# Sliding-window attention and token mixing on one core: exponential over 192 columns per head and key block, scores in 64x64 pieces

## The chip, the cores and the metric

The kernel runs on one core of a Trainium2 chip. The metric is the device time of one execution in microseconds (us); the median of the runs before the change is 136.63 us (136.03 to 137.59, 3 runs). [...]

## The reference

Eight batches, eight heads, 576 tokens, 64 elements per head. A query sees the 128 keys that end at itself, with a bias that falls linearly with the distance and has a slope for each head. The heads' outputs, side by side, are the x of a token mixer.

```python
scores = scale * np.matmul(q, k.transpose(0, 1, 3, 2))
rel = pos[:, None] - pos[None, :]
bias = slopes[:, None, None] * (-np.abs(rel).astype(np.float32))[None, :, :]
mask = (rel >= 0) & (rel < window)          # window = 128
scores = np.where(mask, scores + bias[None], -1000000000.0)
attn = np.exp(scores)                       # divided by its row sum
attn_out = np.matmul(attn, v)
# mixer: x is attn_out as (batch, 576, 512)
W_tok = scale * np.einsum('bsd,btd->bst', x @ w_q, x @ w_k)
mixed = np.einsum('bst,btd->bsd', W_tok, x)
out = np.maximum(mixed, 0.0) @ w_out
```

## The kernel before, in words

**Order.** The order of all work is written out by hand in the table ORDER (line 42). A word such as `QK4.0.1:P:3` names an operation (batch 4, key block 0, half 1 of the heads), its engine (P is PE, A is ACT, V is DVE, G is POOL, S is SP) and, for PE, the PSUM banks; a further number is a count of filler matmuls that go ahead of it. Each engine takes its words from left to right and waits in place for what an operation needs.

**Per batch.** `L...` load q, k and v by POOL's queue (at most some 6 us of transfers at a time), `FQ` the first q heads by SP's. `TW` (batches 0 to 3), `TN` (4 to 7) and `TT` (the last 64 tokens of two batches) transpose q and k on PE; `ETW`, `ETN`, `ETT` on ACT or DVE copy the result from PSUM to `qkT`. `QK` makes the scores, `EXP` (line 608) exponentiates them, `MUL` (line 621) multiplies by exp(bias) with zeros where a key isn't seen, `PV` multiplies by v, and `X` (lines 662 and 663, DVE) divides by the row sum. Then `XT`/`EXT` transpose x, `WK`, `WQ`, `G`, `MX` with `EWK`, `EWQ`, `EG`, `GX`, `RM` on ACT or DVE are the mixer, and `OUT`, `EO`, `DO` multiply by w_out, copy and store.

**Scores (`add_unit`, line 562).** A unit is one key block of 128 keys (g = 0 to 3; g = 3 also holds the last 64 keys) for four heads (u = 0 or 1): 64 units. Keys are the rows of the result, queries its columns. For a full key block and one head a matmul with 64 contraction rows and 128 result rows makes 128 keys by 256 queries: the block's own 128 queries, then the next 128. The two heads e = 0 and 1 of a pair lie in the upper and the lower 64 rows of the array and write to two banks. Of the 256 columns a key uses 128, so half of what `EXP` computes is multiplied by zero. `EXP` writes 1024 columns per unit to `pt` (a ring of 5), `MUL` works in place, for a whole key block (2048 columns) except in batch 0. `EXP` waits until the `PV`s that read the ring's slot five blocks ago are done.

**Forms of the array.** PE's matmuls come in three forms, given in the profile as rows*columns: 128*128 (`PV`, `WK`, `OUT`, filler), 64*128 (`QK`, `TN`, `TT`, `XT`, `MX`) and 128*64 (`TW`, `WQ`, `G`, `OUTb.4`). All matmuls are recorded at line 207, the transposes at 210, the fillers at 908, copies from PSUM mostly at 222, 224, 228 and 230.

Of the kernel before, what the change touches and what calls it, by code (L numbers as in the profile page):

```python
# [1 line left out]

# [16 lines left out]
H = 8  # L19
# [8 lines left out]
NPT = 5  # L28

# [13 lines left out]
FQ1:S FQ0:S Lk0.0:G CQ1:A ones4:V ident:G iota:G dist:V zerop:V zeros:V CQ0:V idh:V perm:V  # L43
Lq0.1:G mask:G bias0:A Lk0.1:G bias1:A ones1:V TW0.0:P:0:15 ETW0.0.0:A ETW0.0.1:V
QK0.1.0:P:0:4:1 QK0.2.0:P:1 EXP0.1.0:A EXP0.2.0:A QK0.0.0:P:2 TW0.1:P:3:1:3 pads:V ones3:V
ones0:V ETW0.1.1:V Lt0.2:G Lt0.3:G ETW0.1.0:A QK0.0.1:P:3:4:0 Lt0.0:G Lt0.1:G QK0.1.1:P:1
QK0.2.1:P:0 EXP0.0.0:A Lq1.1:G Lk1.1:G EXP0.0.1:A EXP0.1.1:A Lq1.0:G EXP0.2.1:A Lk1.0:G Lv0.0:G
Lv0.1:G Lv0.2:G TT0:P:2 ETT0:V ETT1:A QK0.3.1:P:3 QK0.3.0:P:1 Lv0.3:G EXP0.3.0:A TW1.1:P:2:1:0
ETW1.1.0:A MUL0.2.0:V MUL0.0.0:V biasl1:V MUL0.1.0:V MUL0.0.1:V EXP0.3.1:A ETW1.1.1:V
QK1.0.1:P:2:4:0 EXP1.0.1:A QK1.1.1:P:1 Lwq:G Lv0.4:G TW1.0:P:3:2:0 ETW1.0.1:A Lv1.0:G ETW1.0.0:A  # L50
Lwk:G Lq2.1:G biasl0:V MUL0.3.0:V MUL0.1.1:V MUL0.2.1:V MUL0.3.1:V PV0.0:P:2 X0.0:V Lk2.1:G
Lt1.0:G Lv1.1:G PV0.1:P:0:2:0 EXP1.1.1:A Lq2.0:G X0.1:V QK1.1.0:P:3 EXP1.1.0:A PV0.2:P:2 X0.2:V
Lk2.0:G ones2:G QK1.0.0:P:0 EXP1.0.0:A PV0.3:P:1 QK1.3.0:P:2 PV0.4:P:3 X0.3:V XT0.1:P:1
XT0.0:P:0 X0.4:V EXT0.0:V EXP1.3.0:A EXT0.1:A QK1.2.1:P:2 EXP1.2.1:A XT0.2:P:30 EXT0.2:V
MUL1.0:V QK1.2.0:P:1 MUL1.1:V QK1.3.1:P:0 EXP1.3.1:A Lv1.2:G WK0:P:30 MUL1.3:V EWK0:A WQ0:P:20
EWQ0:A Lv1.3:G PV1.0:P:0 X1.0:V G0:P:30 TW2.1:P:2 EXP1.2.0:A PV1.1:P:1 X1.1:V Lv1.4:G Lt1.2:G
EG0:A GX0:A Lt1.1:G MX0.0:P:3 RM0.0:V Lt1.3:G MUL1.2:V MX0.1:P:0 ETW2.1.1:A ETW2.1.0:A MX0.2:P:2
QK2.1.1:P:1 RM0.1:A RM0.2:A QK2.0.1:P:0 XT1.0:P:3 EXT1.0:V EXP2.0.1:A TW2.0:P:2 ETW2.0.0:V
PV1.2:P:0 X1.2:V EXP2.1.1:A ETW2.0.1:A Lq3.0:G QK2.2.1:P:3 PV1.3:P:1 X1.3:V EXP2.2.1:A
QK2.0.0:P:2 PV1.4:P:0 MX0.3:P:3 EXP2.0.0:A RM0.3:A XT1.1:P:1 TT1:P:2 ETT2:A Lk3.1:G Lq3.1:G  # L60
Lk3.0:G Lv2.0:G X1.4:V ETT3:V XT1.2:P:00 EXT1.2:A QK2.2.0:P:3 QK2.1.0:P:2 EXT1.1:V EXP2.2.0:A
QK2.3.0:P:0 WK1:P:10 EXP2.1.0:A QK2.3.1:P:3 MUL2.0:V EWK1:V EXP2.3.1:A MUL2.2:V MUL2.1:V
WQ1:P:11 EWQ1:A Lv2.1:G Lv2.2:G Lv2.3:G G1:P:10 EG1:A Lv2.4:G TW3.1:P:2 ETW3.1.0:V MX1.0:P:1
EXP2.3.0:A MUL2.3:V ETW3.1.1:A RM1.0:A TW3.0:P:3 ETW3.0.1:A ETW3.0.0:A PV2.0:P:2 X2.0:V
QK3.0.1:P:1 EXP3.0.1:A Lk4.1:G Lk4.0:G PV2.1:P:0 X2.1:V QK3.0.0:P:3 GX1:S EXP3.0.0:A Lwo.0:G
PV2.2:P:2 X2.2:V QK3.1.1:P:1 EXP3.1.1:A PV2.3:P:0 X2.3:V QK3.3.0:P:3 EXP3.3.0:A PV2.4:P:2 X2.4:V
Lwo.1:G XT2.0:P:1 EXT2.0:A XT2.1:P:0 EXT2.1:A QK3.3.1:P:3 EXP3.3.1:A Lv3.4:G Lt2.1:G Lwo.2:G
Lwo.3:G Lq4.1:G Lq4.0:G XT2.2:P:20 EXT2.2:V Lk4.2:G Lv3.1:G Lq4.2:G TN4.1.0:P:1 QK3.2.1:P:0
EXP3.2.1:A ETN4.1.0:V Lv3.0:G Lq4.3:G WK2:P:20 EWK2:V Lk4.3:G MX1.1:P:3 RM1.1:V QK3.1.0:P:1
EXP3.1.0:A WQ2:P:21 G2:P:20 EG2:A EWQ2:V MX1.2:P:3 RM1.2:A MX1.3:P:1 RM1.3:V QK3.2.0:P:0 Lv3.2:G  # L70
EXP3.2.0:A GX2:V Lv3.3:G OUT0.3:P:21 EO0.3:A OUT1.3:P:10 EO1.3:A MX2.2:P:0 MX2.0:P:2 MUL3.3:V
RM2.0:A RM2.2:V TN4.0.0:P:3 MUL3.0:V ETN4.0.0:A OUT1.2:P:11 EO1.2:A Lt2.0:G Lk5.1:G Lq5.3:G
MX2.3:P:0 RM2.3:A MX2.1:P:2 MUL3.1:V RM2.1:A QK4.0.1:P:3 EXP4.0.1:A Lk5.0:G OUT0.0:P:10 EO0.0:A
Lq5.1:G Lq5.0:G Lt2.3:G Lt2.2:G PV3.0:P:0 X3.0:V OUT1.0:P:11 EO1.0:A QK4.0.0:P:2 TN4.0.1:P:3
EXP4.0.0:A ETN4.0.1:V TN4.1.1:P:0 ETN4.1.1:A OUT0.2:P:10 EO0.2:A PV3.1:P:3 QK4.1.1:P:2
EXP4.1.1:A Lv4.0:G Lv4.1:G Lk5.2:G Lq5.2:G Lk6.1:G Lk5.3:G Lv4.2:G MUL3.2:V X3.1:V PV3.2:P:0
X3.2:V Lv4.3:G Lv4.4:G QK4.1.0:P:1 QK4.2.1:P:3 EXP4.2.1:A EXP4.1.0:A PV3.4:P:2 OUT2.2:P:00
EO2.2:A X3.4:V MUL4.0:V PV3.3:P:3 X3.3:V TN5.1.0:P:2 ETN5.1.0:A QK4.2.0:P:1 XT3.2:P:01
EXP4.2.0:A EXT3.2:A OUT1.4:P:00 EO1.4:V TN5.0.0:P:2 ETN5.0.0:A TT2:P:3 ETT4:V ETT5:A XT3.0:P:1
EXT3.0:A MUL4.2:V MUL4.1:V XT3.1:P:0 EXT3.1:A QK4.3.1:P:2 QK4.3.0:P:3 EXP4.3.1:A EXP4.3.0:A  # L80
OUT2.0:P:10 PV4.0:P:0 X4.0:V WK3:P:11 PV4.1:P:2 X4.1:V EWK3:A EO2.0:A QK5.0.0:P:3 TN5.0.1:P:0
ETN5.0.1:V EXP5.0.0:A G3:P:11 EG3:A GX3:S MUL4.3:V Lq6.3:G Lv5.0:G WQ3:P:20 EWQ3:A Lv5.3:G
Lq6.1:G Lq6.2:G Lv5.4:G Lq6.0:G Lk6.0:G TN5.1.1:P:0 Lv5.1:G Lv5.2:G ETN5.1.1:A Lk6.3:G Lt3.3:G
QK5.0.1:P:1 XT4.0:P:3 EXT4.0:V PV4.2:P:2 QK5.1.0:P:0 X4.2:V EXP5.0.1:A PV4.4:P:3 X4.4:V
EXP5.1.0:A QK5.2.1:P:1 EXP5.2.1:A PV4.3:P:2 X4.3:V QK5.1.1:P:0 EXP5.1.1:A QK5.3.1:P:3 EXP5.3.1:A
OUT2.1:P:10 EO2.1:A MUL5.0:V MX3.0:P:0 RM3.0:V XT4.1:P:2 EXT4.1:A OUT0.1:P:11 XT4.2:P:10
EXT4.2:A MX3.3:P:0 RM3.3:A MX3.1:P:3 RM3.1:A MUL5.1:V EO0.1:V QK5.2.0:P:2 EXP5.2.0:A WK4:P:10
EWK4:V PV5.0:P:0 X5.0:V QK5.3.0:P:3 EXP5.3.0:A WQ4:P:10 MUL5.2:V G4:P:11 EG4:A GX4:S TN6.1.0:P:0
ETN6.1.0:A MX3.2:P:2 TN6.0.0:P:3 ETN6.0.0:A OUT1.1:P:11 EWQ4:V MUL5.3:V MX4.1:P:3 RM4.1:V
QK6.0.1:P:0 RM3.2:A EO1.1:A PV5.2:P:2 X5.2:V PV5.1:P:1 X5.1:V EXP6.0.1:A TN6.0.1:P:3 ETN6.0.1:A  # L90
# [24 lines left out]
DO6.2:S DO7.3:S EO7.1:V DO7.1:S DO7.0:S DO7.2:S OUT7.4:P:31 EO7.4:A DO7.4:S
# [22 lines left out]
def kernel(  # L138
# [805 lines left out]
```

## Time and profile before

| what | value |
|---|---|
| median of the runs | 136.63 us |
| the profiled execution | 136.72 us |
| its span in the profile | 134.9 us |
| PE busy | 124.2 us, 2353 matmuls |
| ACT busy | 114.8 us, of it `EXP` 63.5 us in 64 instructions |
| DVE busy | 110.0 us, of it `MUL` 38.7 us in 36 instructions |
| POOL busy | 101.0 us |
| granted PE clock | 1.0 |

The execution takes 1.8 us more than its span. Busy time of PE is a union of modelled, overlapping matmuls: a group's row in the timeline lasts until its last result is out, so the distance from one group's start to the next group's start is what a group really takes. "PEld" is the load of the matmul's stationary operand, which runs beside earlier matmuls.

### The profile page before, as it was taken

How to read it: one execution, taken by the hardware profiler on the slowest of the kernel's cores; microseconds unless marked ns; L12 is line 12 of the kernel's file. 1: busy time of each engine (PE TensorE's matmuls, PEld its weight loads, DVE VectorE, ACT ScalarE, POOL GpSimd, SP SyncE). 2: the span in 40 equal slices, each digit the busy share in tenths (PEclk: the TensorE clock that was granted, in tenths of full speed). 3: DMA queues.
4: the chain of work that ended last, by engine and by line, in shares of the span. 5: the costliest groups of instructions: out<-in, count | busy, mean ns of one | idle time of the engine just before them, and what ended most of it. 6: DMA issues, size and time to landing. Idle time of an engine off the chain costs nothing.

```text
span 134.9 us, 5537 instructions
## 1 busy us (share of the span) xinstructions
PE 124.2 (92%) x2353; PEld 81.9 (61%) x2353; DVE 110.0 (82%) x216; ACT 114.8 (85%) x182; POOL 101.0 (75%) x144
## 2 busy tenths in 40 slices
PE   6998599998998989999999999999999999999960
PEld 2355356786777766457688666666766656663420
DVE  3654989899999967988999999999998997973600
ACT  3767978999999989999999999979999897478450
POOL 6995898699497999999999999999880724370000
PEclk9999999999999999999999999999999999999999
DMA  3999999999999999999999999999999999876693
GB/s 109 187 132 178 185 157 161 173 178 125 165 187 151 176 152 146 155 148 148 135 149 145 159 156 148 152 140 147 234 286 232 297 198 329 287 284 254 227 381 91
DMA packets 93319, 25.12 MB, mean 186 GB/s; under 512 B 80368, under 2 KB 89840, under 8 KB 93296
## 3 DMA queue, kind: packets, MB, share of 16 engines
q0 software_dynamic: 89488, 19.28, 152.7%
q1 hardware_dynamic: 3808, 5.51, 12.3%
q8 instruction: 18, 0.29, 0.8%
q14 instruction: 5, 0.04, 0.1%
HBM read 29.62 MB, written 9.44 MB: 289 GB/s over the span
## 4 chain that ended last, share of the span: by engine, by line
PE 65%; ACT 10%; DVE 9%; issue 7%; DMA 4%; POOL 1%; POOLq 0%; DVEq 0%
PE pair L207 53%; PE pair L210 11%; ACT pt L608 5%; DMA natp<-in_k_dram 4%; DVE x L663 3%; DVE pt L621 2%; ACT rm L775 1%; DVE rm L777 1%; ACT qkT L494 1%; DVE inv L662 1%; DVE xtl L663 1%; ACT gs L222 1%; DVE gx L224 1%; ACT wkn L222 1%; ACT gx L222 1%
## 5 line engine op out<-in xcount | busy, mean ns | idle before, releaser
L608 ACT ACTIVATE pt<-pair 128x1024 f16<-128x1024 f32 x64 | 63.5, 1042 | 1.9 <-PE pair L207 1.7
L213 POOL DMA_DIRECT2D vt<-in_v_dram x40 | 36.7, 979 | 5.1 <-DMA natt<-in_k_dram 2.1
L621 DVE TENSOR_TENSOR pt<-pt,bias 128x2048 f16<-128x2048 f16 (+1 forms) x36 | 38.7, 1099 | 0.2
L207 PE MATMUL pair<-wout_sb,rm 128*128 128x512 f16 (+1 forms) x160 | 35.8, 381 | 0.0
L207 PE MATMUL pair<-qkT 64*128 64x256 f16 (+3 forms) x352 | 23.9, 243 | 1.3 <-ACT pt L608 1.0
L207 PE MATMUL pair<-vt,pt 128*128 128x65 f16 x576 | 23.8, 193 | 1.0 <-issue 0.5
L213 POOL DMA_DIRECT2D natp<-in_k_dram x24 | 23.1, 1009 | 1.6 <-POOLq L928 0.8
L207 PEld LDWEIGHTS <-pt 128*128 128x128 f16 x576 | 20.2, 97 | 6.7 <-issue 3.9
L663 DVE TENSOR_TENSOR x<-pair,inv 128x512 f16<-128x512 f32 x32 | 22.1, 692 | 1.1
L213 POOL DMA_DIRECT2D natp<-in_q_dram x23 | 22.3, 1007 | 0.0
L207 PEld LDWEIGHTS <-rm 128*128 128x128 f16 (+1 forms) x160 | 12.4, 100 | 12.9 <-issue 1.7
L222 ACT COPY natp<-pair 128x512 f32<-128x512 f32 x22 | 13.2, 600 | 6.7 <-PE pair L207 6.7
L216 POOL DMA_DIRECT2D out_dram<-natp x16 | 9.3, 614 | 11.2 <-ACT natp L222 10.7
L207 PEld LDWEIGHTS <-qkT 64*128 64x128 f16 x352 | 12.7, 94 | 6.3 <-issue 3.1
L210 PEld LDWEIGHTS <-natp 128*64 128x64 f16 (+1 forms) x512 | 12.6, 102 | 5.0 <-issue 3.5
L777 DVE TENSOR_SCALAR rm<-pair 128x576 f16<-128x576 f32 x14 | 10.4, 752 | 3.3 <-PE pair L207 2.6
L775 ACT ACTIVATE rm<-pair 128x576 f16<-128x576 f32 x18 | 11.4, 668 | 0.9 <-PE pair L207 0.8
L908 PE MATMUL pair<-fill 128*128 128x512 f16 x33 | 10.5, 453 | 1.7 <-DVE fill L350 1.2
L662 DVE RECIPROCAL inv<-pair 128x8 f32<-128x8 f32 (+1 forms) x40 | 8.1, 203 | 2.4 <-PE pair L207 1.6
L228 ACT COPY qkT<-pair 128x512 f32<-128x512 f32 (+1 forms) x18 | 9.2, 542 | 0.8 <-PE pair L210 0.6
L210 PE MATMUL pair<-permh,natp 128*64 128x128 f16 x256 | 8.8, 220 | 1.0 <-DMA natp<-in_k_dram 0.7
L494 ACT COPY qkT<-pair 128x512 f32<-128x512 f32 x11 | 6.2, 593 | 2.2 <-PE pair L210 2.1
(66 smaller groups left out, 154.2 us busy)
## 6 DMA issues: line engine op xcount, KB each, us to landing
vt<-in_v_dram POOLq DMA_DIRECT2D x32, 128.0 KB, 5.3
out_dram<-natp SPq DMA_DIRECT2D x16, 256.0 KB, 2.4
out_dram<-natp POOLq DMA_DIRECT2D x12, 256.0 KB, 4.5
natp<-in_k_dram POOLq DMA_DIRECT2D x8, 256.0 KB, 6.0
natp<-in_k_dram POOLq DMA_DIRECT2D x16, 128.0 KB, 4.8
natp<-in_q_dram POOLq DMA_DIRECT2D x16, 128.0 KB, 4.7
natp<-in_q_dram POOLq DMA_DIRECT2D x7, 256.0 KB, 5.4
out_dram<-osb POOLq DMA_DIRECT2D x4, 256.0 KB, 4.4
```

The source lines that it names most:

```text
L207: hold(nc.tensor.matmul(*a, **k))
L210: hold(nc.tensor.transpose(*a))
L213: hold(nc.gpsimd.dma_start(**k))
L216: i = (nc.gpsimd if eng == "POOL" else nc.sync).dma_start(**k)
L222: hold(nc.scalar.copy(out_ap, in_ap))
L608: nc.scalar.activation(out=pt[:, 1024 * u:1024 * u + 1024], in_=two(s.bank).rearrange("p e c -> p (e c)"), func=AF.Exp, scale=SCALE)
L621: nc.vector.tensor_tensor(out=pt[:, lo:hi], in0=pt[:, lo:hi], in1=bt[:, lo:hi], op=ALU.mult)
L662: nc.vector.reciprocal(out=inv[r], in_=pxv[r, :, :, 64])
L663: nc.vector.tensor_tensor(out=x[r].rearrange("p (g h d) -> p g h d", g=2, h=4), in0=pxv[r, :, :, 0:64], in1=inv[r].unsqueeze(3).broadcast_ ...
L775: hold(nc.scalar.activation(out=out_ap, in_=in_ap, func=AF.Relu, scale=WSCALE))
L777: hold(nc.vector.tensor_scalar(out=out_ap, in0=in_ap, scalar1=0.0, scalar2=WSCALE, op0=ALU.max, op1=ALU.mult))
L908: nc.tensor.matmul(where[:, half, :], fill[:, 0:P], fill, start=True, stop=True)
```

## The change: what it does

In a full key block the first 64 keys need the queries 0 to 190 of the 256, and the last 64 keys the queries 64 to 254. The scores of a head are therefore kept in 192 columns: the upper 64 result rows (first keys) hold queries 128 to 191 in columns 0 to 63 and queries 0 to 127 in columns 64 to 191; the lower 64 rows (last keys) hold queries 128 to 255 in columns 0 to 127 and queries 64 to 127 in columns 128 to 191. Each half has matmuls of its own, 64 contraction rows by 64 result rows, one of 128 and one of 64 columns (for g = 3 the lower half has three of 64): 16 matmuls per unit, 20 for g = 3, where there were 4 (8 or 12 for g = 3). The form 64*64 is new in the program.

`EXP` runs over 768 columns per unit instead of 1024, into a new ring `es` of 4. `MUL` keeps its 2048 results per key block; it reads each head's 192 columns as two overlapping windows of 128 (columns 0 to 127 for the next query block, 64 to 191 for the own one) and writes them to `pt`, so that the table of exp(bias) now has the next block's half first. `MUL`, no longer `EXP`, waits for the `PV`s that read the slot of `pt`; `EXP` waits for the `MUL`s four blocks ago. The constants of the start (`fill`, `ident32`, `wint`, `wm`) now lie in a buffer of the mixer, and the output buffers `osb` are dropped for parts of `natp` and `natt`. `zeros` is gone, and `biasl` is a copy, a memset and a small copy. The whole table ORDER is new; it holds 29 fillers instead of 33.

```diff
-FQ1:S FQ0:S Lk0.0:G CQ1:A ones4:V ident:G iota:G dist:V zerop:V zeros:V CQ0:V idh:V perm:V
+pads:V FQ0:S FQ1:S Lt0.1:G Lk0.0:G ident:G idh:V ones0:V zerop:V ones1:V iota:G Lq0.1:G Lk0.1:G
...
+    e_s = [sb(f"es{i}", [P, H * EW], F16) for i in range(NE)]
...
     def mk_iota(o):
-        nc.gpsimd.iota(wint, pattern=[[1, 256]], base=0, channel_multiplier=-1)
+        nc.gpsimd.iota(wint.rearrange("p (h c) -> p h c", h=2), pattern=[[-P, 2], [1, P]], base=P,
+                       channel_multiplier=-1)
...
+    def sixty(row, n, count, woven):
+
+        lo, wd = 64 * n, 64 * count
+        if woven and n < 8:
+            lo = 256 * (n // 4) + n // 2 % 2 + P * (n % 2)
+            return row[:, lo:lo + 2 * wd - 1:2]
+        return row[:, lo:lo + wd]
...
     def add_unit(b, g, u):
...
-                for kb, qb, c0, wd in cut:
-                    for e in range(2):
-                        r = slice(64 * e, 64 * e + 64)
-                        kk, qq = t[r, hp, 1, :], t[r, hp, 0, :]
-                        dst = ps[:, e, 256 * a + c0:256 * a + c0 + wd]
...
-                        mm(dst, block(kk, kb, w), rhs, start=True, stop=True)
+                steps = []
+                for e in range(2):
+                    r = slice(64 * e, 64 * e + 64)
+                    qq, kk = t[r, hp, 0, :], t[r, hp, 1, :]
+                    dst = ps[:, e, EW * a:EW * a + EW]
+                    low, up = (sixty(kk, 2 * g + i, 1, w) for i in range(2))
+                    n = 2 * g
+                    steps.append([(dst[0:64, 64:192], low, sixty(qq, n, 2, w)), (dst[0:64, 0:64], low, sixty(qq, n + 2, 1, w))])
+                    if g < 3:
+                        steps.append([(dst[64:128, 0:128], up, sixty(qq, n + 2, 2, w)),
+                                      (dst[64:128, 128:192], up, sixty(qq, n + 1, 1, w))])
+                    else:
+                        steps.append([(dst[64:128, 128:192], up, sixty(qq, 7, 1, w)), (dst[64:128, 0:64], up, sixty(qq, 8, 1, w)),
+                                      (dst[64:128, 64:128], sixty(kk, 8, 1, w), sixty(qq, 8, 1, w))])
+                for part in zip_longest(*steps):
+                    for m in part:
+                        if m:
+                            mm(*m, start=True, stop=True)
...
         def ex(o):
-            nc.scalar.activation(out=pt[:, 1024 * u:1024 * u + 1024], in_=two(s.bank).rearrange("p e c -> p (e c)"),
-                                 func=AF.Exp, scale=SCALE)
-
-        x = add(f"EXP{b}.{g}.{u}", ACT(0.905), [s, *oldp], ex, frees=[s])
+            nc.scalar.activation(out=es[:, 768 * u:768 * u + 768].rearrange("p (e c) -> p e c", e=2),
+                                 in_=two(s.bank)[:, :, 0:384], func=AF.Exp, scale=SCALE)
+
+        olde = [mul.get((*divmod(4 * b + g - NE, 4), v)) for v in range(2)]
+        x = add(f"EXP{b}.{g}.{u}", ACT(0.7), [s, *olde], ex, frees=[s])
...
         def ml(o):
             bt = biasw[g == 3].rearrange("p u e a c -> p (u e a c)")
-            nc.vector.tensor_tensor(out=pt[:, lo:hi], in0=pt[:, lo:hi], in1=bt[:, lo:hi], op=ALU.mult)
+            n = (hi - lo) // 256
+            win = es[:, lo // 256 * EW:hi // 256 * EW].rearrange("p (h c) -> p h c", c=EW)[:, :, 0:P]
+            win = bass.AP(win.tensor, win.offset, [win.ap[0], [EW, n], [64, 2], [1, P]])
+            nc.vector.tensor_tensor(out=pt[:, lo + 64:hi + 64].rearrange("p (h x c) -> p h x c", x=2, c=P), in0=win,
+                                    in1=bt[:, lo:hi].rearrange("p (h x c) -> p h x c", x=2, c=P), op=ALU.mult)
...
-                [exps[b, g, v] for v in us] + [(mkb if g < 3 else mkl)[v] for v in us], ml)
+                [exps[b, g, v] for v in us] + [(mkb if g < 3 else mkl)[v] for v in us] + oldp, ml)
```

Three places of the new order, as each engine gets its instructions.

PE in batch 4 before the change, from the last matmul of `OUT1.0` (it reads rm) over a unit of scores, `QK4.0.0` (qkT_77 is its buffer, pair_159 its banks), to the first transpose of `TN4.0.1` (identh with natp):

```order
L207 LDWEIGHTS rm_151
L207 MATMUL pair_158<-wout_sb,rm_151 128x512
L207 LDWEIGHTS qkT_77
L207 MATMUL pair_159<-qkT_77 128x256
...
L210 LDWEIGHTS natp_87
L210 MATMUL pair_160<-identh,natp_87 128x64
```

PE after the change, from the last matmul of `PV3.3` (pt with v) over the same unit's first half, with `QK4.0.1` (pair_153) ahead of `QK4.0.0` (pair_155), to the first matmul of `OUT2.0`:

```order
L213 MATMUL pair_154<-vt_113,pt_120 128x65
L213 LDWEIGHTS qkT_73
L213 MATMUL pair_153<-qkT_73 64x128
...
L213 MATMUL pair_153<-qkT_73 64x64
...
L213 MATMUL pair_155<-qkT_73 64x128
...
L213 MATMUL pair_156<-wout_sb,rm_152 128x512
```

A unit has 16 loads and matmuls where it had 4, and `QK4.0.0`, which stood next to a transpose of its own form 64*128, now stands between a unit of its own form and an `OUT` of another. Counted over the whole table, PE changes its form 125 times before and 134 times after the change.

DVE before, from the last `X` of batch 0 (it writes xtl) over copies of x's transpose (xT) to batch 1's products with the bias and its first `X`:

```order
L663 TENSOR_TENSOR xtl_137<-pair_160,inv 64x512
L230 COPY xT_141<-pair_157 128x4x256
L230 COPY xT_141<-pair_160 128x4x64
L621 TENSOR_TENSOR pt_128<-pt_128,bias_72 128x2048
L621 TENSOR_TENSOR pt_124<-pt_124,bias_72 128x2048
L621 TENSOR_TENSOR pt_126<-pt_126,bias_73 128x2048
L662 RECIPROCAL inv<-pair_157 128x8
```

DVE after, the same stretch:

```order
L660 TENSOR_TENSOR xtl_137<-pair_153,inv 64x512
L619 TENSOR_TENSOR pt_124<-es_125,bias_68 128x2048
L619 TENSOR_TENSOR pt_120<-es_126,bias_68 128x2048
L230 CAST wkn_145<-pair_153 128x320
L230 CAST wqT_143<-pair_153 128x288
L500 TENSOR_SCALAR qkT_73<-pair_154 128x2x256
L659 RECIPROCAL inv<-pair_156 128x8
```

The copies of xT went to ACT, DVE took two copies of the mixer (wkn, wqT) and one of batch 2's q and k (qkT), and two of the four products come behind the first `X`.

POOL at the start before, from the first load of k (natp_80, `Lk0.0`):

```order
L213 DMA natp_80<-in_k_dram 128x4x256
masks.py:197 MEMSET ident_67 128x128
...
L299 IOTA wint 128x256
L213 DMA natp_79<-in_q_dram 128x4x256
L302 AFFINE_SELECT wm<-wm 128x256
L304 AFFINE_SELECT wm<-wm 128x256
L213 DMA natp_80<-in_k_dram 128x4x256
```

POOL after, the same work (natp_76 is k, natp_75 is q, rm_152 holds the constants, natt the last 64 tokens):

```order
L219 DMA natt_91<-in_k_dram 64x8x64
L219 DMA natp_76<-in_k_dram 128x4x256
...
L305 IOTA rm_152 128x256
L219 DMA natp_75<-in_q_dram 128x4x256
L219 DMA natp_76<-in_k_dram 128x4x256
L219 DMA natt_91<-in_k_dram 64x8x64
L219 DMA natt_91<-in_q_dram 64x8x64
L310 AFFINE_SELECT rm_152<-rm_152 128x256
```

A load of 64 tokens has come ahead of the first load of k, and the two selects that make the bias's mask have gone behind the second load of k and two more loads.

More of the change, by code (lines that the diff above doesn't have):

```diff
@@ L28 @@
 NPT = 5
+NE = 4
+EW = 192
 NAT = (0, 1, 2, 3)
@@ L359 @@
     sets = [add(f"ones{i}", {**DVE(0.55), "POOL": (0.9, 0.95)}, [], mk_ones(i)) for i in range(NV)]
-    zeros = add("zeros", {**DVE(0.55), "POOL": (0.9, 0.95)}, [], mk_zeros)
     zerop = add("zerop", {**DVE(0.08 * NPT), "POOL": (0.5, 0.55)}, [], mk_zerop)
@@ L597, in add_unit @@
             need.append(ett[b])
-        s = add(f"QK{b}.{g}.{u}", pe(0.228), need, em, banks=2, mode=1, apart=f"q{b}",
+        s = add(f"QK{b}.{g}.{u}", pe(0.18), need, em, banks=2, mode=3, apart=f"q{b}",
                 member=f"s{b}")
```

219 lines of the change are left out of this document (96 added, 123 removed).

## The prediction

> **What bounds the kernel now.** First the page: the busy shares, the row of PE in the 40 slices, and the chain that ended last.
>
> ```profile
> span 134.9 us, 5537 instructions
> PE 124.2 (92%) x2353; PEld 81.9 (61%) x2353; DVE 110.0 (82%) x216; ACT 114.8 (85%) x182; POOL 101.0 (75%) x144
> PE   6998599998998989999999999999999999999960
> PE 65%; ACT 10%; DVE 9%; issue 7%; DMA 4%; POOL 1%; POOLq 0%; DVEq 0%
> PE pair L207 53%; PE pair L210 11%; ACT pt L608 5%; DMA natp<-in_k_dram 4%; DVE x L663 3%; DVE pt L621 2%; ACT rm L775 1%; DVE rm L777 1%; ACT qkT L494 1%; DVE inv L662 1%; DVE xtl L663 1%; ACT gs L222 1%; DVE gx L224 1%; ACT wkn L222 1%; ACT gx L222 1%
> ```
>
> ACT is the second busiest engine, and the change takes most from it. But the chain runs over PE for 65% of the span and over `EXP` (line 608) for 5%. A share over the whole says little, so next the windows, in two stages (columns: length, then busy PE, PEld, DVE, ACT, POOL, the clock, DMA).
>
> ```profile
> 14.00:49.00 35.00, 31.91 (x771) 24.19 (x772) 32.84 (x61) 33.27 (x50) 29.83 (x45) 1.00 1.81 166
> 49.00:130.00 81.00, 80.22 (x1462) 51.81 (x1457) 70.11 (x114) 71.50 (x117) 60.38 (x79) 1.00 1.74 201
> ```
>
> From 14 to 49 us PE, DVE and ACT are all over 90% busy; none has room for what another gives up. From 49 to 130 us PE is busy for 80.2 of 81 us, while ACT and DVE have some 10 us to spare. So in the long second stage an `EXP` that is shorter frees nothing that PE waits for: what counts there is the length of PE's own list, and in the first stage the shorter of ACT's relief and DVE's.
>
> **ACT.** The price of a shorter `EXP` follows from two of its rows.
>
> ```profile
> L608 ACT ACTIVATE pt<-pair 128x1024 f16<-128x1024 f32 x64 | 63.5, 1042 | 1.9 <-PE pair L207 1.7
> L775 ACT ACTIVATE rm<-pair 128x576 f16<-128x576 f32 x18 | 11.4, 668 | 0.9 <-PE pair L207 0.8
> ```
>
> 448 columns cost 374 ns, 0.835 ns each; 256 columns fewer are 214 ns, and 64 units 13.7 us. The second row's source also lies in two banks with a gap, as the new `EXP`'s does, so I add nothing for the shape. Against it ACT gets four more `RM` and four more `EXT` and gives up four `ETW`, some 2 us. ACT ends near 103 us and is no bound. I count its relief as nothing: in the second stage PE's busy 80.2 of 81 us cover it, in the first DVE's 32.8 of 35. If that cover is thinner than it looks, the most it can give is the 35.0 - 31.9 = 3.1 us of the first stage in which PE is idle; I keep them for the lower end.
>
> **PE: the units of scores.** The timeline of PE gives what groups really take, from start to start.
>
> ```profile
> 56.93 0.30 PE L207 MATMUL pair<-wqT,gs 64*128 64x288 f16 x2
> 57.05 0.40 PE L207 MATMUL pair<-qkT 64*128 64x256 f16 x4
> 57.38 1.04 PE L207 MATMUL pair<-wout_sb,rm 128*128 128x512 f16 x4
> ...
> 59.47 0.39 PE L207 MATMUL pair<-qkT 64*128 64x256 f16 x4
> 59.69 0.63 PE L210 MATMUL pair<-identh,natp 64*128 64x64 f16 x32
> 60.26 1.04 PE L207 MATMUL pair<-wout_sb,rm 128*128 128x512 f16 x4
> 61.13 0.65 PE L207 MATMUL pair<-vt,pt 128*128 128x65 f16 x16
> 42.64 1.08 PE L210 MATMUL pair<-permh,natp 128*64 128x128 f16 x32 [0.37 <-issue]
> 43.66 0.43 PE L207 MATMUL pair<-vt,pt 128*128 128x65 f16 x8
> ```
>
> Four readings. A unit followed by its own form takes 59.69 - 59.47 = 0.22 us; followed by another form 57.38 - 57.05 = 0.33, so a change of form costs about 0.10 us (the four `OUT` matmuls, followed by their own form, take 0.87 or 217 ns each and show no such gap). The 32 transposes of 64 columns take 0.57 - 0.10 = 0.47, or 14.7 ns each: two row halves run at once, 29.4 ns per pair. The 32 transposes of 128 columns in the form 128*64 take 1.02 - 0.10 = 0.92, 28.8 ns each: two column halves run at once, 57.5 ns per pair.
>
> The new form 64*64 is nowhere in this trace. If its four quarters run at once as these halves do, a quarter does, per pair of heads, one piece of 128 and one of 64 columns: 57.5 + 29.4 = 87 ns, and a unit 0.174 us (for g = 3 three pieces of 64 in the lower half: 88 ns, the same). That saves 0.046 us a unit, 64 units 2.9 us. The bounds: the best is the columns alone, 384 of 512 of 0.22 = 0.165, 3.5 us saved. The worst with four at once is that a load and a matmul can't be issued faster than the 14.7 ns of the transposes: 48 units of 16 and 16 of 20 pieces are 1088 x 14.7 = 16.0 us against 64 x 0.22 = 14.1, so 1.9 us lost. If the quarters run only two at a time, a unit takes 0.348 and 8.2 us are lost. I take 0.174: in both halved forms the second matmul of a pair costs nothing visible, and the transposes' 14.7 is explained by their 64 columns, so it is no sign of a limit on issue.
>
> The weights' loads are in the way only if a quarter's load is longer than its matmul.
>
> ```profile
> L210 PEld LDWEIGHTS <-natp 128*64 128x64 f16 x256 | 7.6, 110 | 3.3 <-issue 2.0 <-DMA natp<-in_k_dram 0.8 <-DVE vt L334 0.4
> L210 PEld LDWEIGHTS <-natp 64*128 64x128 f16 x256 | 5.0, 95 | 1.7 <-issue 1.5
> ```
>
> A load of 64 columns in a form with column halves takes 110 ns, one of 128 columns in the whole width 95; both are latencies, and under both the matmuls follow at their own column count. A piece of 64 columns leaves 29 ns for the load of the next; the trace shows no load in column halves under so short a matmul. [...]
>
> **PE: changes of form and fillers.** The words of the order give 134 changes instead of 125: 9 x 0.10 = 0.9 us more. Behind the first transposes 9 fillers stand instead of 13; at the 217 ns of a 512-column matmul that is 0.9 us less, part of it in waits anyway. The two cancel.
>
> **Start and first stage.** POOL issues a load of 64 tokens ahead of the first k.
>
> ```profile
> 1.28 0.89 POOL L213 DMA_DIRECT2D natp<-in_k_dram  x1 [0.83 <-POOLq L928]
> 5.38 0.72 POOL L213 DMA_DIRECT2D natt<-in_q_dram  x1
> 6.51 1.08 PE L210 MATMUL pair<-permh,natp 128*64 128x128 f16 x32
> 4.69 2.56 ACT L314 ACTIVATE bias<-wm 128x256 f16<-128x256 f32 x8 [0.32 <-POOL wm L304]
> 4.61 0.78 POOL L213 DMA_DIRECT2D natp<-in_k_dram  x1
> ```
>
> The first transposes move by 0.7 us, to about 7.2. The second load of k, on which the chain hangs (issued at 4.61, next transposes at 10.7), is issued at about the same time, since it no longer stands behind the mask's selects. The mask comes some 3 us later, the table of exp(bias) with it, and behind that on ACT the first `EXP`, at about 11.5 instead of 8.9. ACT catches up 0.2 us per unit; the eight units of batch 0 and the `ETW` that DVE takes over bring its end from 18.9 to about 18. But DVE makes up batch 0 without a pause either way, and the change gives it the same products, two `ETW` instead of one, and the same small work: I put the end of batch 0's `X` where it is, at 25.9.
>
> ```profile
> 25.20 0.68 DVE L663 TENSOR_TENSOR xtl<-pair,inv 64x512 f16<-64x512 f32 x1
> 25.84 0.89 DVE L230 COPY xT<-pair 128x1024 f16<-128x1024 f16 x2
> 26.65 3.48 DVE L621 TENSOR_TENSOR pt<-pt,bias 128x2048 f16<-128x2048 f16 x3
> 44.27 0.20 DVE L662 RECIPROCAL inv<-pair 128x8 f32<-128x8 f32 x1
> ```
>
> From there to the first `X` of batch 2 DVE needs 18.4 us (44.27 - 25.84) and hardly waits. In the new order it gives up three copies of xT of 0.65, a short one and an `RM` of 0.7 and takes on two `EWQ`/`EWK` more at 0.45 and one `ETW` at 0.65: 0.8 us less, which is the gain of the first stage. A `MUL` keeps its 2048 results and 1.13 us (two of the three in the row above lie 1.13 apart). Its wait for old `PV`s now stands on DVE, with `X` queued behind it and PE's `XT` behind those; before, it stood on ACT. The `PV`s in question are five blocks old, so it costs nothing unless DVE runs far ahead.
>
> **From 49 us on** PE's list sets the end. From the last `PV` of batch 2 on, the old order has 36 units left, 36 x 0.22 = 7.9 us, the new one 33 (three have moved ahead) and one `MX` more (0.13, from 56.93 to 57.05 in the timeline), 33 x 0.174 + 0.1 = 5.8 us; the other operations are the same, with 77 changes of form in each. That is 2.1 us less. The tail behind the last matmul (130.4 to 134.9) is the same.
>
> **Sum.** -0.8 in the first stage and -2.1 in the second, against 134.9: 132.0 in the profile. I take 0.2 back for the later start: -2.7, so 134.0 for the profiled execution's 136.7, and, since that lies 0.1 above the median of 136.63, **133.9 us**.
>
> **The rivals.**
> - *The engines let go of each other.* If ACT's relief closes all of PE's 3.1 idle us in the first stage, the time is 133.9 - 3.1 = 130.8. For it: ACT is 95% busy there. Against it: DVE is at 94% and gets only 0.8 us. Chance 0.10.
> - *The pieces are bound by loads or issue.* A unit stays at 0.22, by the loads, or takes 16 x 14.7 = 0.235 (0.294 for g = 3), by issue. Then the 2.1 us of the second stage go, and by issue up to 1.9 more: 136.0 to 137.9. For it: twice as many instructions per column as in the transposes. Against it: their pairs start together. Chance 0.18.
> - *A floor under the distance of two starts, well above 14.7 ns.* Above 13.8 ns (0.22 / 16) a unit is longer than now, and each further ns costs 1088 x 0.001 = 1.1 us. Against it: the transposes' 14.7, over 32 in a row. Chance 0.01. [...]
> - *The quarters run only two at a time*, at `QK` on PE: 0.348 us a unit, 8.2 us lost over all units in place of the second stage's 2.1 won, 133.9 + 10.3 = 144. It decides as soon as a unit takes more than 0.24, where 33 units lose the 0.6 us that the first stage gains. For it: no row shows four. Against it: both kinds of halves overlap fully. Chance 0.05.
> - *DVE becomes the bound of both stages.* [...] Chance 0.06 for both.
>
> **Chances.** The forecast has 0.60. A measurement of this kernel tells about 1% (1.4 us) from no change. Faster by more: the forecast's share above 1.4 us (0.56) and the first rival (0.10), 0.66. Within 1%: the rest of the forecast (0.04) and most of the pieces' case (0.15), 0.19. Slower: the others, 0.15. The range of 8 in 10 is 130.2 to 137.6; the lower end is the first rival with the unit at its best bound (33 x 0.009 = 0.3 more), rounded down, the upper end the pieces at 14.7 ns, less some of what the first stage may give.
>
> **What would show it.** In the profile after: `EXP` at 0.83 us and ACT near 103 us; a unit of 16 pieces 0.17 to 0.18 us from start to start; changes of form still 0.10; `MUL` at 1.22 us; PE over 95% busy from 49 us on; the first `X` of batch 2 near 43.5. The prediction is wrong if a unit takes 0.22 or more, if `MUL` gets longer, or if PE, with a shorter list, waits more for DVE or a load from 49 us on than now.

## The result, and the profile after

The changed kernel takes **147.04 us** (median of 4 runs, 146.45 to 149.02) against 136.78 us before (4 runs beside them). The ratio is 1.073 with a 95% interval of 1.065 to 1.082: 7.3% slower, where the prediction said 133.9 us and 2% faster. The profiled execution below took 149.02 us, some 2 us more than the other three.

The page of the changed kernel: span, busy shares, the rows of PE and of its clock in 40 slices, the queue of the instructions (packets, MB, share), the chain, and the two groups whose cost was forecast.

```profile
span 147.2 us, 6978 instructions
PE 125.7 (85%) x3085; PEld 86.9 (59%) x3085; DVE 109.7 (74%) x207; ACT 104.6 (71%) x183; POOL 102.4 (70%) x156
PE   6974699768968757799999899999999799999950
PEclk9999689999999999789999999999999999999998
q8 instruction: 24, 0.39, 1.0%
PE 64%; DMA 9%; issue 8%; DVE 7%; ACT 6%; POOL 2%; DVEq 0%; ACTq 0%; POOLq 0%
L602 ACT ACTIVATE es<-pair 128x768 f16<-128x768 f32 x64 | 49.7, 818 | 10.6 <-PE pair L213 9.8
L619 DVE TENSOR_TENSOR pt<-es,bias 128x2048 f16<-128x2048 f16 (+1 forms) x36 | 38.5, 1098 | 0.1
```

`EXP` takes 0.818 us where 0.83 was forecast, ACT comes to 104.6 us (103), `MUL` keeps its 1.10. What the change was to do to these engines it did. But they now wait: PE is busy for 125.7 of 147.2 us, and its row has holes (6, 8, 7, 5, 7, 7, from 40 to 63 us) where it had eights and nines. The instructions' own queue moved 24 packets of 0.39 / 24 MB = 16 KB. The same row of the kernel before:

```profile
q8 instruction: 18, 0.29, 0.8%
```

Next the two stages, moved by the 6 to 8 us that the first became longer:

```profile
14.00:57.00 43.00, 33.83 (x1084) 27.45 (x1083) 34.08 (x63) 30.98 (x50) 38.63 (x60) 0.96 1.87 161
57.00:142.00 85.00, 81.54 (x1871) 54.36 (x1868) 70.12 (x117) 65.98 (x119) 52.75 (x71) 0.98 1.46 178
```

In the first PE is idle for 9.2 us (before: 3.1), and DVE and ACT for about as much or more: none of them is the bound there. So the question is what PE waits for. The timeline of PE over one of the holes:

```profile
51.91 0.65 PE L213 MATMUL pair<-qkT 64*64 64x128 f16 x18
54.34 0.36 PE L213 MATMUL pair<-qkT 64*64 64x128 f16 x14 [1.78 <-issue]
54.64 0.66 PE L213 MATMUL pair<-vt,pt 128*128 128x65 f16 x16
55.22 0.38 PE L213 MATMUL pair<-qkT 64*64 64x128 f16 x20
55.54 0.66 PE L213 MATMUL pair<-vt,pt 128*128 128x65 f16 x16
56.13 0.37 PE L213 MATMUL pair<-qkT 64*64 64x128 f16 x16
56.43 0.66 PE L213 MATMUL pair<-vt,pt 128*128 128x65 f16 x16
57.02 0.30 PE L213 MATMUL pair<-wqT,gs 64*128 64x288 f16 x2
57.29 0.66 PE L216 MATMUL pair<-identh,x 64*128 64x64 f16 x28
59.72 0.26 PE L216 MATMUL pair<-identh,x 64*128 64x64 f16 x4 [1.77 <-issue]
```

PE stops in the middle of a group, between matmuls that wait for no other engine ("issue"): after 18 pieces of a unit, then after 28 of 32 transposes. Count the matmuls between the two holes: 14 + 16 + 20 + 16 + 16 + 16 + 2 + 28 = 128. Each is a load and a matmul, so 256 instructions, which at 16 KB per packet is one packet of the queue above (64 bytes each). The counts agree: 6170 loads and matmuls are 24.1 times 256, and the queue moved 24 packets; before, 4706 are 18.4 times 256, and it moved 18. Call such 256 instructions a block (the expectations below say page). In the whole trace seven gaps of more than 0.4 us stand where one block ends and the next begins, exactly 256 instructions or a multiple of it apart, 9.76 us in all, the longest 2.03; before, two such gaps make 1.35 us. (A gap is counted here from the start of one PE instruction to the start of the next, some 0.2 us more than PE's idle time; the expectations below use an earlier count, 9.4 and 1.2.) One of the seven, 1.20 us of idle time ahead of 43.59, the profile puts down to a copy by DVE, but that copy had ended at 43.03.

That PE waits for the packet itself is shown by the packets' own times in the trace of after (us):

| PE starts a block | a packet starts | it has landed | PE starts the next block | gap ahead of that |
|---|---|---|---|---|
| 27.47 | 31.13 | 32.09 | 33.39 | 1.60 |
| 43.59 | 46.45 | 47.40 | 48.69 | 1.34 |
| 48.69 | 51.92 | 52.88 | 54.34 | 2.03 |
| 54.34 | 57.36 | 58.29 | 59.72 | 1.96 |
| 87.78 | 89.56 | 90.50 | 92.39 | none |

Ahead of each of the seven gaps one packet starts, 1.7 to 3.7 us after PE has gone into the block; it takes 0.9 to 1.1 us, and 1.1 to 1.6 us after it has landed PE goes on. In the last row PE still has work when the packet has landed, and nothing waits. So in these rows the next block is on its way only while PE works on the present one. All 71 gaps of over 0.4 us between two blocks, in the 17 traces of this study, end 1.1 to 1.7 us after a packet has landed. What differs from gap to gap is mainly the time until the packet starts.

Where the time came from, by the starts of the first matmul of `PV0.0`, of `PV2.0` and of the last one (us; in brackets the gaps over 0.4 us between blocks):

| stage of PE's list | before | after | difference |
|---|---|---|---|
| up to `PV0.0` | 20.32 (0) | 22.96 (0) | +2.6 |
| `PV0.0` to `PV2.0` | 23.34 (0.7) | 27.68 (4.9) | +4.3 |
| `PV2.0` to the last matmul | 86.36 (0.7) | 91.03 (4.9) | +4.7 |

The last matmul starts 11.7 us later than before, and 8.4 of them are such gaps. The other executions of the same instructions further down (after_old_order, after_mended, after_ahead5) have 7.0 to 7.6 us of them. A smaller part is the clock: it was granted at 0.50 for 3.4 us from 60.5 us on, 0.8 us behind the gap of 1.96 that ends at 59.72. The windows of PE and the timeline there:

```profile
60.60:63.80 3.20, 3.20 (x50) 2.62 (x51) 3.20 (x5) 2.15 (x4) 3.20 (x5) 0.50 2.20 142
60.57 1.23 PE L213 MATMUL pair<-wk_sb,xT 128*128 128x64 f16 x20
```

At a granted clock of 0.50 `WK` lasts 1.23 us, where it takes 0.74 to 0.76 at full clock. There are two such stretches of 3.4 us each (from 16.2 and from 60.5 us), so at most 2 x 1.7 = 3.4 us.

### The profile page after: what moved, and what is told of

Its sections match the earlier page's. It is cut to its first block, busy times and chain, and to the rows that moved or that the text cites. A ratio compares the mean times of both kernels' runs of the same rounds, so it can differ in the third digit from the quotient of the medians.

```text
span 147.2 us, 6978 instructions
## 1 busy us (share of the span) xinstructions
PE 125.7 (85%) x3085; PEld 86.9 (59%) x3085; DVE 109.7 (74%) x207; ACT 104.6 (71%) x183; POOL 102.4 (70%) x156
## 4 chain that ended last, share of the span: by engine, by line
PE 64%; DMA 9%; issue 8%; DVE 7%; ACT 6%; POOL 2%; DVEq 0%; ACTq 0%; POOLq 0%
PE pair L213 52%; PE pair L216 11%; DMA natp<-in_k_dram 5%; DMA gx<-gs 4%; ACT es L602 2%; DVE pt L619 2%; DVE qkT L500 2%; POOL natp L219 1%; DVE x L660 1%; PE pair L905 1%; DVE xtl L660 1%; ACT rm L772 1%; DVE qkT L236 1%; ACT xT L234 1%; DVE inv L659 1%
## 5 line engine op out<-in xcount | busy, mean ns | idle before, releaser
L602 ACT ACTIVATE es<-pair 128x768 f16<-128x768 f32 x64 | 49.7, 818 | 10.6 <-PE pair L213 9.8
L619 DVE TENSOR_TENSOR pt<-es,bias 128x2048 f16<-128x2048 f16 (+1 forms) x36 | 38.5, 1098 | 0.1
L222 POOL DMA_DIRECT2D out_dram<-natp x20 | 11.4, 588 | 26.4 <-ACT natp L228 18.5
L213 PE MATMUL pair<-qkT 64*64 64x64 f16 (+1 forms) x1088 | 20.1, 207 | 6.0 <-issue 2.9
L219 POOL DMA_DIRECT2D natp<-in_q_dram x23 | 20.7, 922 | 2.3 <-DMA vt<-in_v_dram 1.8
L213 PEld LDWEIGHTS <-qkT 64*64 64x64 f16 x1088 | 15.2, 109 | 11.5 <-issue 7.5
L772 ACT ACTIVATE rm<-pair 128x576 f16<-128x576 f32 x22 | 13.6, 654 | 2.7 <-PE pair L213 2.5
L500 DVE TENSOR_SCALAR qkT<-pair 128x512 int32<-128x512 int32 x9 | 6.1, 689 | 11.0 <-PE pair L216 11.0
L905 PE MATMUL pair<-rm 128*128 128x512 f16 x29 | 10.4, 495 | 1.2 <-DVE rm L355 1.2
L234 ACT COPY xT<-pair 128x512 f32<-128x512 f32 (+1 forms) x17 | 7.9, 490 | 4.5 <-PE pair L216 4.4
```

Source lines behind the costliest of these rows:

```text
L213: hold(nc.tensor.matmul(*a, **k))
L219: hold(nc.gpsimd.dma_start(**k))
L222: i = (nc.gpsimd if eng == "POOL" else nc.sync).dma_start(**k)
L234: hold(nc.scalar.copy(out_ap.bitcast(FP32), in_ap.bitcast(FP32)))
L602: nc.scalar.activation(out=es[:, 768 * u:768 * u + 768].rearrange("p (e c) -> p e c", e=2), in_=two(s.bank)[:, :, 0:384], func=AF.Exp, sca ...
L619: nc.vector.tensor_tensor(out=pt[:, lo + 64:hi + 64].rearrange("p (h x c) -> p h x c", x=2, c=P), in0=win, in1=bt[:, lo:hi].rearrange("p ( ...
```

## The experiments

The theory: PE's program now asks for its instructions faster than they are fetched. 732 more matmuls are 1464 more instructions, nearly half of them ahead of 62 us. From 22 to 58 us five of the blocks of 256 take PE only 3.4 to 3.9 us, one 4.3; with the gap ahead of the next each takes 4.6 to 5.9. The seventh takes 5.5 us, and no gap of over 0.4 us follows it. The rivals: the new order of the work, the new form and piece size, or the later start. The kernel before was run beside each of them, with medians of 136.8 to 137.1 us.

### More instructions, nothing else: before_split64

```diff
-                        mm(dst, block(kk, kb, w), rhs, start=True, stop=True)
+                    for c in range(0, wd, 64):
+                        for e in range(2):
...
+                            mm(dst, block(kk, kb, w), rhs, start=True, stop=True)
```

> The kernel before, with its scores' matmuls cut into pieces of 64 columns (16 per unit, 672 matmuls more in all); columns, form 64*128, EXP, MUL and order are as before. Theory (PE waits for its next 256 instructions, and the gaps grow with the number of instructions per us): the gaps without a semaphore at every 256th PE instruction, 1.2 us in the trace of before, become at least 4 us in all, and the time 141 to 146 us. Rival (the change lost by its new order and form, not by the number of instructions): only the pieces' own pitch counts, 14.7 ns against 13.8, about 1 us, so at most 138.5 us.

Measured: 144.07 us, ratio 1.044 (1.030 to 1.058). Nine gaps over 0.4 us at every 256th instruction, 9.35 us in all. More instructions alone make the kernel before as slow as the theory said; form, order, `EXP` and `MUL` are the old ones.

### Fewer instructions, nothing else: after_one192

```diff
-                    steps.append([(dst[0:64, 64:192], low, sixty(qq, n, 2, w)), (dst[0:64, 0:64], low, sixty(qq, n + 2, 1, w))])
...
+                    steps.append([(dst[0:64, :], low, qs[0])])
+                    steps.append([(dst[64:128, :], up, qs[1])])
```

> The changed kernel with one matmul of 192 columns per quarter instead of 128 + 64 (8 per unit instead of 16 or 20; the rotated layout, and the last 64 keys of g = 3, are left out, so the scores are not the reference's). Columns, form, order, EXP and MUL stay, PE has 544 matmuls fewer. Theory (instruction supply): most of the 9.4 us of gaps at every 256th PE instruction go, under 3 us stay, and the time is 136 to 140 us. Rival (order or waits): the gaps are not the cause, 145 us or more.

Measured: 136.99 us, ratio 1.001 (0.996 to 1.006); one gap of 0.67 us is left, and 19 packets on the queue. So 10.0 of the 10.3 us that the change lost went with 576 matmuls, 1152 instructions (3085 matmuls against 2509; the expectation's 544 is a miscount), while columns, form and order stayed. The timeline of PE at its one gap:

```profile
51.20 0.35 PE L213 MATMUL pair<-wk_sb,xT 128*128 128x64 f16 x6
52.02 0.58 PE L213 MATMUL pair<-wk_sb,xT 128*128 128x64 f16 x14 [0.48 <-issue]
```

### The order apart from the operations: after_old_order

The table ORDER is the one before, without the word `zeros`.

> The changed kernel's operations in the order table of the kernel before (without the word zeros). Theory (instruction supply): as many PE instructions as the change, so gaps of 6 to 10 us at every 256th of them and 143 to 149 us, whichever order. Rival (the new order is what lost): near the prediction's 134 us, at most 138.

Measured: 147.48 us, ratio 1.071 (1.060 to 1.082), six gaps, 7.12 us. So the new order isn't what lost.

### Fewer loads in flight: after_ahead3, after_ahead5

```diff
-AHEAD = 6.0
+AHEAD = 3.0
```

> The changed kernel with at most some 3 us of loads in flight instead of 6 (AHEAD = 3.0). If the fetch of instructions waits behind the loads' transfers, the gaps shrink from 9.4 us to about half and the time falls by 3 to 5 us, to 142 to 144. If the fetch has a latency of its own, the gaps stay, and the time is the same or longer, since loads land later: 146 to 150.

Measured: 169.32 us, ratio 1.221 (1.206 to 1.237). One gap of 0.44 us is left, but PE now waits for the loads:

```profile
PE pair L213 <- DMA vt<-in_v_dram: 8.1, 12, 1.2
PE pair L216 <- DMA natp<-in_q_dram: 7.5, 8, 2.6
```

This was read too simply in the expectation: both of its cases came true at once, and since the waits make the blocks of 256 longer, the gaps could have gone for that reason alone. The value between:

> The changed kernel with at most some 5 us of loads in flight instead of 6. If the fetch stands behind the loads in flight, the gaps shrink a little before the loads become late: 144 to 147. If loads are already the tighter side at 5 us (3 us gave 169): 148 to 153, with fewer gaps and more waits for loads.

Measured: 147.58 us, ratio 1.072 (1.060 to 1.084), seven gaps, 7.04 us: no gain. Whether loads slow the fetch needed a measurement of its own.

### The fetch by itself: probe_quiet, probe_loads, probe_loads_big

Behind the last matmul of the kernel before stand 768 more that nothing reads; the other two add loads beside them.

```diff
+    for i in range(768):
+        c, r = slice(64 * (i // 2 % 2), 64 * (i // 2 % 2) + 64), slice(64 * (i % 2), 64 * (i % 2) + 64)
+        nc.tensor.matmul(pairs[2][c, i % 2, 0:64], identh[r, 0:64], identh[r, 0:64], start=True, stop=True)
```

> The kernel before, with 768 matmuls of 64x64 by 64 columns added behind its last one (1536 PE instructions, six times 256, nothing reads them); only the last stores run beside them. Theory: in a dense run the time per 256 instructions is set by their supply once what is in store is used up; with little other traffic I expect 2 to 3.5 us per 256. Rival (supply costs nothing without a wait): 128 pieces at 10 to 14 ns, 1.3 to 1.8 us per 256, no gaps.

The timeline of PE:

```profile
130.65 1.63 PE L913 MATMUL pair<-identh 64*64 64x64 f16 x171
134.81 1.92 PE L913 MATMUL pair<-identh 64*64 64x64 f16 x128 [2.54 <-issue]
138.27 1.92 PE L913 MATMUL pair<-identh 64*64 64x64 f16 x128 [1.53 <-issue]
141.72 1.92 PE L913 MATMUL pair<-identh 64*64 64x64 f16 x128 [1.53 <-issue]
145.18 1.92 PE L913 MATMUL pair<-identh 64*64 64x64 f16 x128 [1.53 <-issue]
148.91 1.38 PE L913 MATMUL pair<-identh 64*64 64x64 f16 x85 [1.80 <-issue]
```

Blocks of exactly 128 matmuls start 3.46 us apart (138.27 - 134.81, and again twice), though each is started within 1.7 us: 13.5 ns per instruction, with hardly any other traffic. The packets' times divide the 3.46 us: about 1.05 until the packet starts, 1.05 for the packet, 1.35 until PE goes on. All this is at a granted clock of 0.50; at full clock the changed kernel has one block (101.85 to 105.17) that takes 3.3 us with a gap of 0.15, parted as 1.0, 1.0 and 1.3. A unit of the changed kernel wants 32 instructions in its 0.2 us, 6 ns each.

> As probe_quiet, with 24 loads of v (into buffers that nothing reads any more) issued by POOL beside the 768 matmuls. If the fetch stands behind the loads' transfers: 4 to 6 us per 256 instructions, as in the changed kernel's dense pages, against the 2 to 3.5 of probe_quiet. If loads don't matter: the same as probe_quiet.

```profile
130.71 1.60 PE L916 MATMUL pair<-identh 64*64 64x64 f16 x171
138.72 1.92 PE L916 MATMUL pair<-identh 64*64 64x64 f16 x128 [6.41 <-issue]
145.74 1.92 PE L916 MATMUL pair<-identh 64*64 64x64 f16 x128 [5.10 <-issue]
152.49 1.92 PE L916 MATMUL pair<-identh 64*64 64x64 f16 x128 [4.82 <-issue]
156.21 1.92 PE L916 MATMUL pair<-identh 64*64 64x64 f16 x128 [1.81 <-issue]
```

Beside the loads of v a block takes 7.7, 7.0 and 6.8 us, twice as long and more than expected; once they have landed, 3.7. The packet itself still takes 1.0 to 1.1 us; it starts 4.0 to 5.4 us after PE has gone into the block.

> As probe_loads, but the 24 loads bring the same bytes in rows of 1 KB instead of 256 bytes (a quarter of the packets). If the number of packets is what the fetch stands behind: near 3.5 to 4.5 us per 256 instructions. If bytes in flight: 6.5 us or more, as in probe_loads.

```profile
135.95 1.92 PE L917 MATMUL pair<-identh 64*64 64x64 f16 x128 [5.16 <-issue]
140.50 1.93 PE L917 MATMUL pair<-identh 64*64 64x64 f16 x128 [2.63 <-issue]
145.60 1.93 PE L917 MATMUL pair<-identh 64*64 64x64 f16 x128 [3.17 <-issue]
149.60 1.92 PE L917 MATMUL pair<-identh 64*64 64x64 f16 x128 [2.08 <-issue]
```

With rows of 1 KB a block takes 4.6, 5.1 and 4.0 us after a first one of 6.4, although more bytes move: from 140 to 147 us the core's DMA moved 229 GB/s, in probe_loads 174. That speaks for the number of packets, rather than the bytes, as what the fetch stands behind. Each probe ran only once, so this isn't settled.

### Where the instructions stand, and how many: split64_b23, split64_b67, split128

> The kernel before with the scores in 64-column pieces in batches 2 and 3 only (160 matmuls more, 320 PE instructions). Columns, form and order as before. Theory (what counts is how many instructions fall into the time of one fetch, while loads run): here the pages of 256 already take only 5 us, so the gaps grow by 2 to 3 us and the time is 138.5 to 140.5. Rival (each further instruction costs the same wherever it stands): 0.24 of what before_split64 lost, 1.7 us, 138.5 or less, and the same as split64_b67.

Measured: 141.87 us, ratio 1.037 (1.030 to 1.044): 5 us for 320 instructions, twice the forecast and three times the rival's. Most of it is one gap, where the same group ran through before. The timeline of split64_b23, then of the kernel before:

```profile
39.00 0.40 PE L207 MATMUL pair<-wk_sb,xT 128*128 128x64 f16 x8
42.40 0.82 PE L207 MATMUL pair<-wk_sb,xT 128*128 128x64 f16 x12 [2.99 <-issue]
```

```profile
38.75 0.74 PE L207 MATMUL pair<-wk_sb,xT 128*128 128x64 f16 x20
```

256 instructions in 3.56 us stand ahead of that gap of 3.18 us, whose packet started 4.2 us after PE had gone into the block; the clock is at half for 6.8 us from 41.1 us on.

> The same cut in batches 6 and 7 only (176 matmuls more), where the loads run out and the pages take longer. Theory: the gaps stay within 1 us of before, 136.5 to 138. Rival (the same cost wherever): as split64_b23.

Measured: 139.5 us as the median of only 4 runs from 137.1 to 144.7, too far apart for a size. The profile, of the longest, has gaps of 1.9 and 2.0 us behind two of the cut blocks (from 97 to 108 us), and longer ones than before at 41 and 48 us, where nothing was cut. The shortest run lies within the forecast, so a loss in the later stage is not shown as a rule, but the stage is not safe either. And the same gap at the same place can be 0.7 or 1.8 us: at 43 us the packet started 3.1 us after PE had gone into the block in the kernel before and 4.3 us after it here.

> The kernel before with the scores' matmuls in pieces of at most 128 columns (224 matmuls more, 448 PE instructions, spread over all batches). Theory: a unit is 16 instructions per 0.22 us; the dense pages come down to some 4.5 us and the gaps to 1.5 to 3 us: 137 to 138.5. If the cost were in proportion to the instructions added (before_split64: 7 us for 1344): 139.1.

Measured: 137.63 us, ratio 1.005 (1.001 to 1.009), one gap of 0.97 us. 448 instructions, spread out, cost 0.7 us, where 160 matmuls in the dense stage cost 5: the price isn't per instruction but per block that comes too soon.

### What the change is worth without these gaps: one192_mended, after_mended, one192_old_order, one192_gx5_dve

after_one192 has the change's columns, `EXP` and order and hardly any gaps, and still gains nothing. Its trace shows a later start and a wait of `MX5.3` for a transfer (`GX5` by SP). Both were put back:

```diff
-pads:V FQ0:S FQ1:S Lt0.1:G Lk0.0:G ident:G idh:V ones0:V zerop:V ones1:V iota:G Lq0.1:G Lk0.1:G
-Lt0.3:G Lt0.2:G perm:V dist:V CQ1:A CQ0:V TW0.0:P:0:15 ETW0.0.0:V mask:G ETW0.0.1:A
+FQ1:S FQ0:S Lk0.0:G ident:G iota:G dist:V idh:V zerop:V Lq0.1:G mask:G Lk0.1:G Lt0.1:G
+Lt0.3:G Lt0.2:G CQ1:A CQ0:V perm:V TW0.0:P:0:15 ETW0.0.0:V ETW0.0.1:A ones0:V ones1:V pads:V
...
-G5:P:20 EXP6.2.1:A EG5:V GX5:S
+G5:P:20 EXP6.2.1:A EG5:V GX5:A
```

> after_one192 (it leaves out the rotated layout and the last 64 keys of g = 3) with two things put back: the start as in the kernel before (the first k ahead of the load of 64 tokens, dist and mask early, ones and pads late on DVE), and GX5 on ACT instead of a transfer by SP. If these two waits hold what is missing to the prediction once the fetch is out of the way, the first EXP comes near 9.5 us instead of 11.7, the 1.1 us wait of MX5.3 goes, and the time is 134 to 135.5. If the time lies elsewhere: 136 to 137.

Measured: 136.67 us, ratio 0.998 (0.993 to 1.003), not the 134 to 135.5 expected. The first `EXP` starts at 10.87, not near 9.5, and `PV0.0` at 21.13 instead of 22.02, but two gaps at blocks come to 1.98 us, and the 1.0 us wait stands at `OUT4.3` now, for the bank that `GX5` reads.

> The changed kernel with the same two things put back (start, GX5 on ACT). By the theory the gaps at every 256th PE instruction stay at 7 to 10 us, so at most 2 us are gained: 145 to 147. If the order of the start were the main cause: under 140.

Measured: 148.26 us, ratio 1.079 (1.067 to 1.092): the real change gains nothing from it, and five gaps of 7.58 us stay.

> after_one192's operations (it leaves out the rotated layout and the last 64 keys of g = 3) in the order table of the kernel before. If the new order's own waits take back what the operations gain: the start as before, and 133.5 to 135.5 us. If the operations gain nothing without the waits for instructions either: 136 to 137.5.

Measured: 137.98 us, ratio 1.008 (1.005 to 1.010). The old order makes these operations slower, not faster, a gap of 1.22 us between two blocks included; the first of the two cases expected is out, and the new order is worth some 1 to 2 us to them.

> one192_mended with GX5 on DVE instead of ACT (there the wait of 1.0 us had moved to OUT4.3, whose bank GX5 reads). If that wait is the missing microsecond: 135 to 136. If not: 136.3 to 137, as one192_mended.

Measured: 135.75 us, ratio 0.992 (0.989 to 0.995). That is what the change's columns and order, with these two mends, are worth when PE gets its instructions: 1.1 us of the 2.7 forecast. Two things differ from one192_mended, the word `GX5:V` and the gaps between blocks (one of over 0.4 us, 0.44, instead of 1.98 us); which of them gave the 0.9 us isn't shown. The rotated layout needs its two pieces per quarter, so no kernel of this study has both, and none that does the whole work beats the kernel before.

## Why the prediction was wrong

**The step that failed** is the sentence on which the second stage rested: that what counts there is "the length of PE's own list". The list was priced by columns, pieces and changes of form, and no term asked whether 6170 loads and matmuls reach PE as fast as 4706 do. The runs showed in its place that they don't: with 4706 the gaps between blocks are 1.35 us, with 6170 they are 7.0 to 9.8 us, and with 5018 (after_one192) 0.67. The row was on the page (18 packets of instructions), and the trace of before held two such gaps, one of them in a row that the prediction quotes, `TW` at 42.64 with "0.37 <-issue". It was passed over.

**"It is no sign of a limit on issue."** For the pieces themselves this was right: a unit with a change of form behind it takes 0.30 us, by the timeline of after (the third row holds three units):

```profile
41.40 0.37 PE L213 MATMUL pair<-qkT 64*64 64x128 f16 x16
41.70 0.45 PE L216 MATMUL pair<-identh,x 64*128 64x64 f16 x16
43.81 0.81 PE L213 MATMUL pair<-qkT 64*64 64x128 f16 x56
44.55 0.68 PE L213 MATMUL pair<-xT,wq_sb 128*64 128x288 f16 x8
```

Three units in a row take 0.74 us, where one of 16 pieces alone takes 0.30 and one of 20 pieces (two of the three are such) 0.32: two changes of form fewer are 0.20 us less, so a change costs 0.10. Without it a unit takes 0.20 us, against 0.174 forecast and 0.22 before; four quarters do run at once (the first four pieces of these three units start within 10 ns), and the loads, 109 ns each where a piece follows the last after 9 to 14 ns, are hidden for the most part. No run shows the 0.22 us at which the rival of the pieces keeps a unit by the loads; the runs showed 0.20 in its place. But a limit on the rate of one unit and a limit on 256 instructions in a row are two things. The rival of the pieces stopped at the first: its worst case, 137.9 us, charged 14.7 ns per piece to the unit alone. probe_quiet gives 27 ns per piece (2 x 13.5, at a granted clock of 0.50) behind the 342 instructions that ran before the first wait.

**The first stage.** The start was forecast 0.7 us late and lost behind DVE. The first `EXP` started at 10.93 (11.5 forecast), but `PV0.0` came 2.6 us late, with the first stretch at half clock (16 to 20 us) in it, and that was not made good. From batch 0's last `X` to the first of batch 2, DVE's busy time did fall, as the windows of before and of one192_gx5_dve show:

```profile
25.84:44.27 18.43, 17.36 (x421) 13.59 (x418) 18.13 (x28) 18.22 (x31) 14.68 (x24) 1.00 1.82 162
```

```profile
25.54:44.03 18.49, 17.25 (x443) 13.65 (x440) 17.55 (x26) 16.84 (x31) 15.91 (x32) 1.00 1.81 161
```

DVE is busy for 17.55 instead of 18.13 us, 0.6 of the 0.8 forecast, but the stretch is as long as before: what DVE gave up it waited for PE (0.5 us in two waits). With PE at 91%, DVE at 94% and ACT at 95%, three engines share that stage before the change, and relief of one or two is worth little.

**The second stage** was forecast 2.1 us shorter. In one192_gx5_dve it is 85.3 us from `PV2.0` to the last matmul, against 86.4: 1.1. Its 38 units there take 9.5 us against 12.3 for the old 40, including the changes of form; part of that is given back at `MX` and at the transposes `TN`, 1.2 and 1.0 us longer from start to start. That the other operations take what they took in the old order was an assumption without a row. (The lower end of the range, 130.2, doesn't follow from its own terms either: 130.8 - 0.3 is 130.5.)

**What was right:** `EXP`, ACT's total, `MUL` with its overlapping windows, 0.10 us per change of form, four quarters at once. All of them are prices of single operations; ACT's total came to 104.6 us, not 103. The rival that the quarters run only two at a time gave 144 us, near the result, for a reason that the trace refutes.

**Still open:** why the packet of a block starts 1.0 us after PE has gone into the block in one place and over 4 in another (the probes point to the loads' packets ahead of it), and what PE does in the 1.1 to 1.7 us after the packet has landed. The clock's share (at most 3.4 us) wasn't taken apart by a run of its own.

## What to carry to other kernels

Before a change that cuts matmuls into smaller ones, count the instructions, load and matmul each, and look for the stretch where 256 of them take PE the least time. In these kernels PE waited for its program behind blocks of 5.1 us and less beside loads, though not behind each (from 88 to 102 us the changed kernel ran blocks of 4.6 to 4.9 us without a gap); in no trace of this study did a block take less than 3.3 us. Such waits mostly stand in the middle of a group, name no engine, and lie a multiple of 256 instructions apart; two small ones (0.67 and 0.68 us) stood in the trace of before already. A gain of engines that another one covers should be weighed against what the change adds to the covering one in instructions, not only in time.

## What the runs showed of the hardware that was not expected

- PE's instructions come in blocks of 256 (16 KB), one per 3.46 us in a quiet run, 4.0 to 6.4 beside loads of 1 KB rows, 6.8 to 7.7 beside loads of 256 byte rows. One packet comes per block, nearly always after PE has gone into the block ahead of it. In probe_quiet PE had run at over 7 us per 256 just before, and still only 171 of the added matmuls (342 instructions) ran before the first wait.
- In the trace of after the granted clock was 0.50 for 3.41 us from 16.16 and from 60.53 us on, although no gap of PE ahead of them was longer than 2.03 us: in the 3.41 us ahead of each PE was busy for 0.43 and 0.48 of the time.
- In the form 64*64, when four quarters take turns, a piece of 64 columns is followed by the next start after 9 ns on average and a piece of 128 columns after 14 ns (trace of after, at full clock).
